# One gated load, two units later: the q load of batch 3 in pass w = 1 of a linear-attention and PReLU feed-forward kernel

## The chip, the cores and the metric

The kernel runs on one core of a Trainium2 chip. The metric is the device time of one execution in microseconds (us), the median of several runs on the same chip. Profiles come from one profiled execution each; a time such as "at 68.26" is us from the start of its span. PE is the matmul engine, PEld its weight loads, DVE the vector engine, ACT the scalar engine, POOL the GpSimd engine, SP the sync engine, which here only issues DMAs.

## The reference

For each of 8 batches and 8 heads of 64, with 576 rows each, attention without softmax is computed, then normalised over the head's 64 columns:

```
kv  = einsum('bhsd,bhse->bhde', k, v)
o   = einsum('bhsd,bhde->bhse', q, kv)
o   = o / sqrt(mean(o*o, -1) + 1e-6) * g_norm
x   = o laid out as (8*576 = 4608 rows) x (8*64 = 512 columns)
h   = x @ w_in                     # 512 -> 2048
g   = max(h, 0) + alpha * min(h, 0)
out = g @ w_out                    # 2048 -> 512
```

Inputs and output are float32. The kernel works in float16 with float32 accumulation.

## The kernel before, in words

**Blocks and passes.** The 4608 rows are cut into nine blocks of 512 rows, w = 0 to 8, each of four tiles of 128 rows. A block does not line up with a batch of 576 rows: block 2 (rows 1024 to 1535) takes its rows from batches 1 and 2, block 3 (1536 to 2047) its first 192 rows from batch 2 and the rest from batch 3. Block 0 is done by a start-up part of its own. The main loop at the end of the function (`for w in range(1, NW)`) makes passes w = 1 to 8, each of 16 units u. The change is in pass w = 1, the second of the nine blocks, here called loop 2 where they are counted from one.

**What a unit does.** Unit u of pass w multiplies xt of block w (the transposed attention output, four chunks of 128 x 512) with one 128-column block of w_in: four matmuls of 128 x 512 into a PSUM bank `h_ps` (`m1_mm`, L600). ACT takes Relu(-h) into `m_sb` (`m1_neg`, L609), DVE forms gt = h + beta * m_sb (`m1_sum`, L615). Then come matmuls of the second product (`prod_mm`, L796; yX, yY, yZ). They form a Strassen-like scheme on 2 x 2 halves, so DVE also adds and subtracts halves of gt (`s_sum`, L731 to L737) and of results (L828, L838, L840), and ACT copies results out (L824, L834). Results go to `y_sb` buffers, four in rotation, and are stored from there (L655) by POOL or SP.

**Attention of the next block.** Beside its own units, pass w makes xt of block w + 1, in `attention(w + 1, u)`, by a table `ROW_AT` written out by hand: at which unit the products k-transposed times v of a batch are formed (`row_kv`, L1122, with the masked copy L1134), at which the row matmuls of each tile (`rows_mm`, L499), the squares (L562 or L556), the reciprocal root (L572) and the scaling into `x_rows` on DVE (`rows_norm`, L580). Right behind L580, SP issues a DMA transpose of the tile into xt (L585). For block 2 the scalings of tiles 0, 1 and 3 stand at units 4, 9 and 9 of pass 1. Tile 2 of block 2 is made in column form (`cols_mm` L512, L522, L527, L534, and at unit 13 L541) and needs no transpose.

**The first unit of a pass.** From block 2 on, unit 0 is cut in two (`m1_cols`, L631): first the columns of tiles 0 to 2 (384), then, after second-product matmuls where the schedule has any, the columns of tile 3 (128). So the last transpose of a block may land a little after the pass has begun. In pass 2 the schedule has none of these between the two parts.

**q, k and v.** k and v are loaded by POOL with a cast to float16 into `kst` and `vst` (L176), with the last 64 rows of a batch in separate tiles (L198, `ksb`, `vsb`, `qsb`). From batch 3 on, q is loaded by `load_q` in four parts of 128 rows into `qst` (L185) and a fifth of 64 rows into `qsb` (L198). Each part is then transposed by an SP DMA into `qt_sb` (`dma_t`, L380); there are two `qt_sb`, for even and odd batches. Row matmuls read `qt_sb` as weights. The parts of batch 2 are transposed in pass 1 at units 0, 3, 3, 14 and 15; all five parts of batch 3 at units 0 to 2 of pass 2.

**What sets the order.** Each engine works through its instructions in the order in which this program writes them, and waits there for what they need. SP issues, in pass 1 and at the start of pass 2: the transposes of block 2's tiles, the last two parts of batch 2's q, the five of batch 3's q, then six stores of block 0's results that were held back (put at unit 5 of pass 2), then block 3's tiles. POOL issues loads and part of the stores. A load is held back by a gate: a copy of one element of a gt tile on POOL (L1186), which POOL cannot pass before DVE has written that gt. The table `LOADS` says at which unit of which pass a load is written, and its gate reads the gt of the unit before:

```python
        q, k, v = (11, 1, 1) if w == 1 else (12, 3, 5)
        for nm, at in (("q", q), ("k", k), ("v", v)):
            when = LOADS.setdefault((w + at // NF, at % NF), [])
            if at > 1 or w == 1:
                when.append(("gate", w, at - 1))
            when.append((nm, w + 2))
```

With w = 1 this is batch 3, with q at unit 11 behind the gt of unit 10; k and v stand at unit 1. In the later passes q stands at unit 12, k and v at units 3 and 5. Batch 2 is loaded by the start-up part.

Of the kernel before, what the change touches and what calls it, by code (L numbers as in the profile page):

```python
# [17 lines left out]
def kernel(  # L18
# [1168 lines left out]

    LOADS = {}
    for w in range(1, B - 2):
        q, k, v = (11, 1, 1) if w == 1 else (12, 3, 5)  # L1190
        for nm, at in (("q", q), ("k", k), ("v", v)):
            when = LOADS.setdefault((w + at // NF, at % NF), [])
            if at > 1 or w == 1:
                when.append(("gate", w, at - 1))
            when.append((nm, w + 2))
# [50 lines left out]
    w = NW - 1  # L1246
# [62 lines left out]
```

## Time and profile before

| | us |
|---|---|
| median of 3 runs | 274.43 |
| lowest and highest of them | 274.05, 274.45 |
| the profiled execution | 274.92 |
| its span, first to last instruction | 273.1 |
| PE, DVE, ACT busy | 265.7, 217.3, 156.4 |

The granted PE clock is 0.999 of full speed over the span. In the lists below, a line of a timeline has the start, the length and the instruction (with xN, N of them merged into one line), and in square brackets the idle time of its engine just before it with what ended that idle time. A line of the waits has the total, the number and the longest of the waits of one line on one cause. A line of the chain has start, length and what the time went to. The start and length of a DMA instruction on POOL or SP are those of its issue; when the data has landed is a time of its own, and "issue to landing" is the distance.

### The profile page before, as it was taken

The numbers are of one execution on the slowest core, as the hardware profiler recorded it, in microseconds if no ns is written. First come the engines' busy times: TensorE is split into PE (matmuls) and PEld (weight loads), VectorE is DVE, ScalarE is ACT, GpSimd is POOL, SyncE is SP. The second block draws the span as 40 slices with busy tenths as digits, with TensorE's granted clock in tenths as the row PEclk, the third lists the DMA queues.
The fourth block names the chain that finished last, engine by engine and source line by source line (L and its number), as shares of the span: only waits on it lengthen the run. The fifth ranks groups of instructions, "written<-read, shape, count | busy, mean of one in ns | idle before, by whom it ended". The sixth has DMA issues, their size and how long they took to land.

```text
span 273.1 us, 6175 instructions
## 1 busy us (share of the span) xinstructions
PE 265.7 (97%) x2286; PEld 168.5 (62%) x2286; DVE 217.3 (80%) x413; ACT 156.4 (57%) x532; POOL 87.6 (32%) x134
## 2 busy tenths in 40 slices
PE   7899999999799999999999999999999999999995
PEld 3354444456566676666666666676666666666684
DVE  6459658999768986998699869986998889778964
ACT  3467576785468546764675468546854864443410
POOL 8773461606251545154514341440110011101100
PEclk9999999999999999999999999999999999999999
DMA  8999999999989899959995999595051122211123
GB/s 160 197 202 202 195 199 193 178 182 108 161 159 204 132 166 148 153 113 172 135 144 130 151 135 158 137 143 111 19 134 43 41 44 90 61 40 40 40 77 119
DMA packets 91571, 35.59 MB, mean 130 GB/s; under 512 B 62980, under 2 KB 89748, under 8 KB 91540
## 3 DMA queue, kind: packets, MB, share of 16 engines
q0 software_dynamic: 57872, 23.83, 69.1%
q1 hardware_dynamic: 32628, 10.34, 22.4%
q10 hardware_dynamic: 1040, 1.02, 1.2%
q8 instruction: 18, 0.29, 0.4%
q14 instruction: 13, 0.11, 0.2%
HBM read 36.71 MB, written 9.44 MB: 169 GB/s over the span
## 4 chain that ended last, share of the span: by engine, by line
PE 79%; DMA 14%; DVE 2%; issue 1%; POOL 1%; ACT 1%; POOLq 0%
PE h_ps L600 35%; PE yY L796 15%; PE yZ L796 9%; PE yX L796 9%; DMA w_out_sb<-in_moe_w_out_dram 5%; PE y L643 4%; DMA xt<-x_rows 4%; DMA w_in_sb<-in_moe_w_in_dram 3%; DMA qst<-in_q_dram 2%; PE h_ps L631 2%; PE kv_ps L1122 2%; PE or_ps L499 2%; DVE gt L615 1%; DVE x_rows L580 1%; PE yZ L791 1%
## 5 line engine op out<-in xcount | busy, mean ns | idle before, releaser
L600 PE MATMUL h_ps<-xt,w_in_sb 128*128 128x512 f16 x540 | 136.2, 379 | 0.0
L609 ACT ACTIVATE m_sb<-h_ps 128x512 f32<-128x512 f32 x144 | 86.7, 603 | 81.9 <-PE h_ps L600 61.4
L615 DVE SCALAR_TENSOR_TENSOR gt<-m_sb,beta_sb,h_ps 128x512 f16<-128x512 f32 x144 | 106.2, 743 | 24.1 <-ACT m_sb L609 21.3
L600 PEld LDWEIGHTS <-w_in_sb 128*128 128x128 f16 x540 | 51.2, 98 | 39.4 <-issue 0.2
L655 POOL DMA_DIRECT2D out_dram<-y_sb x32 | 20.6, 646 | 123.3 <-DVE y_sb L838 57.1
L796 PEld LDWEIGHTS <-s 128*128 128x128 f16 x496 | 48.3, 98 | 11.3 <-DVE s L733 0.3
L796 PEld LDWEIGHTS <-gt 128*128 128x128 f16 x384 | 37.5, 98 | 23.2 <-issue 0.2
L796 PE MATMUL yX<-w_out_sb,gt 128*128 128x256 f16 x256 | 44.6, 273 | 0.0
L796 PE MATMUL yY<-wsum,s 128*128 128x256 f16 x256 | 35.2, 273 | 0.0
L562 ACT ACTIVATE sq_sb<-or_ps 128x64 f16<-128x64 f32 x144 | 30.9, 256 | 2.6 <-PE or_ps L499 2.6
L562 ACT ACTIVATION_READ_ACCUMULATOR sq_sb<-or_ps 128x1 f32 x144 | 30.3, 242 | 0.0
L580 DVE TENSOR_TENSOR x_rows<-or_ps,rstd_r 128x512 f16<-128x512 f32 x27 | 18.4, 684 | 1.0 <-ACT rstd_r L572 1.0
L828 DVE TENSOR_TENSOR u<-yY,p 128x512 f32<-128x512 f32 x16 | 11.0, 689 | 9.0 <-PE yY L796 9.0
L185 POOL DMA_DIRECT2D qst<-in_q_dram x20 | 17.7, 901 | 1.0 <-issue 1.0
L796 PE MATMUL yY<-wsum,gt 128*128 128x256 f16 x128 | 17.6, 272 | 0.0
L796 PE MATMUL yZ<-wsum,s 128*128 128x256 f16 x120 | 17.5, 272 | 0.0
L796 PE MATMUL yZ<-w_out_sb,s 128*128 128x256 f16 x120 | 16.7, 273 | 0.0
L643 PE MATMUL y<-w_out_sb,gt 128*128 128x512 f16 x64 | 16.3, 379 | 0.1
L731 DVE TENSOR_TENSOR s<-gt 128x512 f16<-128x512 f16 x32 | 13.3, 418 | 0.1
L733 DVE TENSOR_TENSOR s<-s,gt 128x512 f16<-128x512 f16 x32 | 12.8, 420 | 0.4
L737 DVE TENSOR_TENSOR s<-gt,s 128x512 f16<-128x512 f16 x32 | 12.7, 418 | 0.0
L735 DVE TENSOR_TENSOR s<-gt 128x512 f16<-128x512 f16 x32 | 12.4, 417 | 0.0
(107 smaller groups left out, 233.1 us busy)
## 6 DMA issues: line engine op xcount, KB each, us to landing
out_dram<-y_sb POOLq DMA_DIRECT2D x16, 256.0 KB, 2.7
kst<-in_k_dram POOLq DMA_DIRECT2D x7, 512.0 KB, 8.0
vst<-in_v_dram POOLq DMA_DIRECT2D x6, 512.0 KB, 7.9
qst<-in_q_dram POOLq DMA_DIRECT2D x20, 128.0 KB, 4.5
w_out_sb<-in_moe_w_out_dram POOLq DMA_DIRECT2D x8, 256.0 KB, 10.9
out_dram<-y_sb SPq DMA_DIRECT2D x5, 256.0 KB, 2.6
w_in_sb<-in_moe_w_in_dram POOLq DMA_DIRECT2D x2, 512.0 KB, 9.9
qst<-in_q_dram POOLq DMA_DIRECT2D x2, 512.0 KB, 11.9
```

The costliest lines, as they stand in the source:

```text
L185: nc.gpsimd.dma_start(out=st[:, t, :, :], in_=srcs["q"][b, :, t * P : (t + 1) * P, :].rearrange("h p d -> p h d"),)
L562: nc.scalar.activation(out=sq[:, half, j], in_=o_ps[:, half, j], func=AF.Square, accum_out=ssq[:, half, j : j + 1],)
L580: nc.vector.tensor_tensor(out=xr[:].rearrange("p j h d -> p h j d"), in0=o_ps, in1=rstd[:].unsqueeze(3).to_broadcast([P, 2, NPAIR, D]), op ...
L600: nc.tensor.matmul(out=h_ps[:], lhsT=w_in_blk(c, g), rhs=xts[w][:, c, :], start=(c == 0), stop=(c == NC - 1),)
L609: nc.scalar.activation(out=neg[w, g][:], in_=h_ps[:], func=AF.Relu, scale=-1.0)
L615: nc.vector.scalar_tensor_tensor(out=gts[w, i][:, r, :], in0=neg.pop((w, g))[:], scalar=beta_sb[:, g : g + 1], in1=h_ps[:], op0=ALU.mult, ...
L643: nc.tensor.matmul(out=y[:], lhsT=gt_cols(w, g, a * P, (a + 1) * P), rhs=w_out_blk(g), start=(n == 1), stop=(n == NF),)
L655: engs[store_turn[0] % len(engs)].dma_start(out=dst, in_=src)
L731: nc.vector.tensor_add(out=t[:], in0=a21, in1=a22)
L733: nc.vector.tensor_sub(out=t[:], in0=sums[w, 1, k][:], in1=a11)
L737: nc.vector.tensor_sub(out=t[:], in0=a12, in1=sums[w, 2, k][:])
L796: nc.tensor.matmul(out=bank, lhsT=lhs, rhs=rhs, start=fresh, stop=(c == NK - 1), skip_group_check=True,)
```

## The change

In the table `LOADS`, q of batch 3 is written at unit 13 of pass 1 instead of unit 11, and its gate reads the gt of unit 12 instead of unit 10. All that hangs on it is the gate copy, the four loads at L185 and the one at L198. Nothing else on POOL stands between units 11 and 13. In the program's order the load now stands after the last scaling of block 2 (unit 13) and before the transposes of batch 2's last two parts (units 14 and 15).

```diff
     LOADS = {}
     for w in range(1, B - 2):
-        q, k, v = (11, 1, 1) if w == 1 else (12, 3, 5)
+        q, k, v = (13, 1, 1) if w == 1 else (12, 3, 5)
         for nm, at in (("q", q), ("k", k), ("v", v)):
             when = LOADS.setdefault((w + at // NF, at % NF), [])
             if at > 1 or w == 1:
                 when.append(("gate", w, at - 1))
             when.append((nm, w + 2))
```

## The prediction

> **What bounds the kernel now.** I read the page first, then the waits of the matmul queue, then the chain, and last the timelines of PE, SP, POOL and DVE around the place of the change. Times are microseconds from the start of the profiled execution.
>
> ```profile
> PE 265.7 (97%) x2286; PEld 168.5 (62%) x2286; DVE 217.3 (80%) x413; ACT 156.4 (57%) x532; POOL 87.6 (32%) x134
> ```
>
> PE is busy for 97% of the span, so only two things shorten this kernel: fewer matmuls, or fewer holes between them. The edit changes no matmul. The holes are few; this is the whole list of what PE waited for, total, times, longest:
>
> ```profile
> PE h_ps L631 <- DMA xt<-x_rows: 1.6, 1, 1.6
> PE warm_ps L297 <- DVE y_sb L119: 1.5, 1, 1.5
> PE kv_ps L403 <- ACT qt_sb L361: 0.8, 1, 0.8
> PE ssq_ps L460 <- ACT sq_sb L444: 0.2, 1, 0.2
> ```
>
> The last three are in the first 15 us. The largest is one wait of 1.6 at L631, where unit 0 of a pass multiplies the last 128 columns, those of tile 3. The chain and PE's timeline place it at the start of pass w = 2:
>
> ```profile
> 63.95 5.83 DMA xt<-x_rows
> 69.78 0.04 issue
> ```
>
> ```profile
> 67.45 0.81 PE L631 MATMUL h_ps<-xt,w_in_sb 128*128 128x384 f16 x4
> 69.83 0.38 PE L631 MATMUL h_ps<-xt,w_in_sb 128*128 128x128 f16 x4 [1.56 <-DMA xt<-x_rows]
> ```
>
> The first 384 columns end at 68.26; then PE stands for 1.56 until the transpose of tile 3, issued at 63.95, has landed at 69.78, 5.83 after its issue. POOL and SP show what it shared the DMA engines with:
>
> ```profile
> 62.87 0.18 POOL L1186 COPY gate_sb<-gt 1x1 f16<-1x1 f16 x1 [8.04 <-DVE gt L615]
> 63.36 3.58 POOL L185 DMA_DIRECT2D qst<-in_q_dram  x4 [0.32 <-issue]
> 66.91 0.73 POOL L198 DMA_DIRECT2D qsb<-in_q_dram  x1
> 73.33 2.14 POOL L655 DMA_DIRECT2D out_dram<-y_sb  x4 [5.70 <-ACT y_sb L834]
> ```
>
> ```profile
> 55.67 9.50 SPq L585 DMA_TRANSPOSE xt<-x_rows  x3
> 65.22 3.19 SPq L380 DMA_TRANSPOSE qt_sb<-qsb  x2
> 68.66 5.39 SPq L380 DMA_TRANSPOSE qt_sb<-qst  x4
> 74.15 1.21 SPq L380 DMA_TRANSPOSE qt_sb<-qsb  x1
> 75.41 4.26 SPq L655 DMA_DIRECT2D out_dram<-y_sb  x6
> ```
>
> The q load goes out at 63.36, 0.59 ahead of the transpose. In the DMA view by slices of 1 us, POOL's queue has 1 packet in 64 to 65, 437 in 65 to 66, 553, 804 and 959 in the next three; SP's queue has 46, 1, 391, 140 and 116. So the transpose finds the engines taken when its packets come up, at about 66.
>
> **The change, part by part.** Nothing is added or removed, and the order of instructions on every engine stays the same. The copy at L1186 now reads gt of unit 12 instead of unit 10, and five loads stand behind it on POOL (four of L185, one of L198).
>
> *How far it moves.* DVE's L615 for units 10 and 11 fills 61.99 to 63.39; unit 12 is the one at 63.64, 0.74 long, so done at 64.38. With the 0.14 that the copy took after its gt before, it starts at about 64.52, which is 1.65 later. The loads are then issued from 65.01 to 69.3 instead of 63.36 to 67.64, and their packets begin near 66.7 instead of 65.0. "Two units" is 1.65 us here: the load is issued 1.06 behind the transpose instead of 0.59 ahead.
>
> *What the transpose then takes.* No row has exactly this distance, so I bound it. Below: 2.4, issue to landing, for the same transpose of the pass that has no q load (203.12). Above: the passes where a q load is issued 0.16 behind the same transpose, 3.8 (120.12) and 3.6 (175.41). That is landing at 66.4 to 67.8. PE needs it at 68.26, so all of the 1.56 goes, with 0.5 to spare. I take the end near 3.6, since a load is near.
>
> The row first: most of tile 3's data packets are through by 67.5 (391 + 140 of SP's packets by 68, some of them the next transpose's), yet it counts as landed at 69.78. The Trainium skill (DMA: Bandwidth & Descriptors, Queues, rings and completion order) says that an engine takes turns among its queues by packet, and that a completion increment lands only after all earlier writes of that engine, those of other queues too. By turns alone the wait should have been shorter than measured; by the rule on increments, q writes still hold a landing if they begin before it. By the first the sum keeps 1.56, by the second part of it can stay; this is the first rival below.
>
> *What moves up behind the hole.* PE's next work is kv (k and v landed by 63.4) and unit 1. DVE is the nearest limit:
>
> ```profile
> 68.07 0.75 DVE L731 TENSOR_TENSOR s<-gt 128x512 f16<-128x512 f16 x2
> 68.74 0.75 DVE L733 TENSOR_TENSOR s<-s,gt 128x512 f16<-128x512 f16 x2
> 70.88 0.75 DVE L615 SCALAR_TENSOR_TENSOR gt<-m_sb,beta_sb,h_ps 128x512 f16<-128x512 f32 x1 [1.39 <-ACT m_sb L609]
> ```
>
> The sums end at 69.49 whatever PE does, so DVE moves up by 1.39, not 1.56. Unit 2's matmuls move from 72.86 to 71.3 and need gt of unit 0, then done at 70.2; the sums that PE takes from about 72.2 are done at 71.0 and 71.8. So PE is not held, and the 0.17 is made up where DVE idles later (1.10 at 78.14, 1.13 at 80.35). I count 1.5, between 1.39 and 1.56.
>
> *What becomes late.* On POOL the next instruction is the store at 73.33, which waits for ACT; the loads end at 69.3, so nothing queues. On SP the four transposes of L380 each wait for their own part of q: in the rows they start within 0.15 us of its landing. They move by 1.65 to about 70.3 to 75.8, and the six stores behind them from 75.41 to 77.1, ending at 81.3. SP's next is block 3's first transpose, 84.18 before and 82.6 when moved up with PE: 1.3 to spare. PE's first use of the new q is the row matmul of unit 4, 78.27 before and 76.7 after. Batch 3's first transpose landed 5.0 after its issue at 68.66, at 73.7; 1.65 later is 75.3, so 1.4 to spare. Parts 1 and 2 of q (transposed by 74.6, then 76.2) are used from 80.25, then 78.7: 2.5 to spare. The cover of the move is this slack; without it each us costs one us on PE.
>
> Two y_sb buffers change places as well: the sum at L840 near 95.4 takes the one stored by POOL from 73.33 (landed by 79.2), the copy at L834 of pass 2 the one stored last by SP (landed by 85.7, then 87.3). Both are needed after 93, so this costs nothing.
>
> *Later passes* keep their distances, since their gates, norms and loads follow PE. Block 3's tile 3 is issued at 92.53; its increments end at 96.8 and its use is at 98.07, so 1.3 is left.
>
> **Sum.** 0 + 1.5 gained, 0 lost. The profiled execution took 274.92 (span 273.1 and 1.8 around it); the median is 274.43, 0.49 below. I take the difference from both: 273.4 for the one, **272.9** for the median.
>
> **Rivals.**
>
> 1. *The hole only shrinks.* The load still begins 1.6 ahead of PE's need, and its writes hold the landing. For it: 5.83 beside it before, and the 4.5 of the transpose at 231.08, which had no q load. Against: 3.6 and 3.8 with the load closer. At 5.0 (batch 3's first transpose, mid-load) tile 3 lands at 68.95 and 0.7 of the hole stays: gain 0.8, 273.6.
> 2. *The hole moves.* The DMA work of 65 to 90 starts 1.65 later while PE comes 1.56 earlier, and the next such place, block 3's tile 3 with 1.3 to spare, stalls. All 1.56 lost there needs 2.9 of delay. For it: the DMA engines are nearly full from 80 to 89. Against: they carry nothing from 90.3 to 91.5. Time 274.4, no change.
> 3. *Slower: the row matmuls of unit 4 wait for q.* The place is PE's L499; it decides when batch 3's first transpose lands after 76.7. The longest landing of a transpose beside a large load in this trace is 8.9 (issued 55.67, under the k and v loads). Issued at 70.3 it would land at 79.2, PE would stand for 2.5, and the net is 0.95 worse: 275.4. Against: the rows beside this very load are 5.0, 3.9 and 3.2.
>
> **How the numbers follow.** Forecast 0.76, own range 272.5 to 273.4 (1.39 to 1.56 gained, 0.4 either way for scatter and small leftovers; the three runs lie within 0.4). Rival 1 0.10, rival 2 0.06, rival 3 0.08. The range takes in the forecast and rival 1, 272.4 to 273.9, and leaves out 0.14. A measurement of this kernel can tell 0.2%, 0.55 us, from no change: faster means below 273.9, which the forecast and rival 1 give, 0.86; same 0.06; slower 0.08.
>
> **What would show it.** The L1186 copy near 64.5 and the loads from 65.0 show the move. L631's wait gone from PE's list, and tile 3 landing within 4.0 of its issue, show the gain; a landing of 4.5 to 5.5 is rival 1. A wait of L631 near 96 is rival 2; a wait of L499 near 77 is rival 3. It would be wrong altogether if tile 3 landed as late as before with the load out of its way: then the k and v loads, or the transposes among themselves, were the cause.

## The result, and the profile after

The changed kernel takes 273.38 us (median of 22 runs), the kernel before 274.36 in the same comparison: ratio 0.9962, 95% interval 0.9949 to 0.9975, so 1.0 faster. Two later comparisons of the same two kernels gave 0.9984 (0.9964 to 1.0004) and 0.9978 (0.9961 to 0.9995), that is 0.4 and 0.6; the ratio is that of the means, and the first of these two intervals reaches 1. The profiled execution after has a span of 271.7 against 273.1.

The page's first line, after: no busy time has changed by more than 0.2, but PE's same work fills 98% of a shorter span.

```profile
PE 265.6 (98%) x2286; PEld 168.5 (62%) x2286; DVE 217.3 (80%) x413; ACT 156.2 (58%) x532; POOL 87.4 (32%) x134
```

All that PE waited for, after (total, times, longest). The wait of L631 is gone; what is left is start-up:

```profile
PE warm_ps L297 <- DVE y_sb L119: 1.5, 1, 1.5
PE kv_ps L403 <- DMA vst<-in_v_dram: 1.1, 1, 1.1
PE ssq_ps L460 <- ACT sq_sb L444: 0.2, 1, 0.2
```

PE's timeline after, where the two parts of unit 0 now run into each other and are listed as one line of eight matmuls:

```profile
67.85 1.04 PE L631 MATMUL h_ps<-xt,w_in_sb 128*128 128x384 f16 x8
```

POOL and SP after. The start-up part ran 0.40 later in this execution (this L631 was at 67.45 before), so 64.92 stands for 64.52:

```profile
64.92 0.18 POOL L1186 COPY gate_sb<-gt 1x1 f16<-1x1 f16 x1 [9.68 <-DVE gt L615]
65.42 3.59 POOL L185 DMA_DIRECT2D qst<-in_q_dram  x4 [0.32 <-issue]
72.01 2.14 POOL L655 DMA_DIRECT2D out_dram<-y_sb  x4 [2.31 <-ACT y_sb L834]
```

```profile
70.21 5.24 SPq L380 DMA_TRANSPOSE qt_sb<-qst  x4
75.56 2.42 SPq L380 DMA_TRANSPOSE qt_sb<-qsb  x1
78.03 3.79 SPq L655 DMA_DIRECT2D out_dram<-y_sb  x6
82.85 9.55 SPq L585 DMA_TRANSPOSE xt<-x_rows  x4
```

Tile 3's transpose was issued at 64.37 and landed at 66.79, 2.42 later instead of 5.83. In the list of issues with their time to landing, window 65 to 66, it stands as:

```profile
xt<-x_rows SPq DMA_TRANSPOSE x1, 2.4
```

What each queue moved between 67 and 68, after (packets, MB, share of the 16 engines): it is the first slice of 1 us with packets of the q load, and tile 3 has landed by then.

```profile
q0 software_dynamic: 344, 0.04, 68.0%
q1 hardware_dynamic: 101, 0.03, 19.6%
```

Set side by side by matmul, PE's starts are 0.40 behind before's up to L631, then 1.32 ahead: 1.72 from the hole. This is more than the 1.56 of idle time, because the end of a matmul in the profile lies about 0.17 behind the point at which the next one can start: before, the fifth matmul of L631 could have started at 68.09 and started at 69.83. They stay 1.3 ahead up to pass 8, where before lost another 0.28 to a late landing at L631 that a second trace of before does not have. The end is 1.59 ahead.

### The profile page after: what moved, and what is told of

Same layout as the page of the kernel before. It is cut to its first block, busy times and chain, and to the rows that moved or that the text cites. A ratio compares the mean times of both kernels' runs of the same rounds, so it can differ in the third digit from the quotient of the medians.

```text
span 271.7 us, 6175 instructions
## 1 busy us (share of the span) xinstructions
PE 265.6 (98%) x2286; PEld 168.5 (62%) x2286; DVE 217.3 (80%) x413; ACT 156.2 (58%) x532; POOL 87.4 (32%) x134
## 4 chain that ended last, share of the span: by engine, by line
PE 94%; DMA 3%; POOL 1%; issue 1%; ACT 0%; DVE 0%; POOLq 0%
PE h_ps L600 44%; PE yY L796 16%; PE yX L796 10%; PE yZ L796 10%; PE y L643 5%; DMA vst<-in_v_dram 3%; PE h_ps L631 2%; PE kv_ps L1122 2%; PE or_ps L499 2%; PE ssq_ps L460 1%; PE yZ L791 1%; PE h_ps L945 1%; POOL kst L168 0%; PE ot_ps L437 0%; PE kv_ps L418 0%
## 5 line engine op out<-in xcount | busy, mean ns | idle before, releaser
L615 DVE SCALAR_TENSOR_TENSOR gt<-m_sb,beta_sb,h_ps 128x512 f16<-128x512 f32 x144 | 106.3, 744 | 22.4 <-ACT m_sb L609 19.3
L185 POOL DMA_DIRECT2D qst<-in_q_dram x20 | 17.7, 906 | 1.0 <-issue 1.0
```

What stands on the lines that cost most here:

```text
L185: nc.gpsimd.dma_start(out=st[:, t, :, :], in_=srcs["q"][b, :, t * P : (t + 1) * P, :].rearrange("h p d -> p h d"),)
L615: nc.vector.scalar_tensor_tensor(out=gts[w, i][:, r, :], in0=neg.pop((w, g))[:], scalar=beta_sb[:, g : g + 1], in1=h_ps[:], op0=ALU.mult, ...
```

## The experiments

My theory: the hole is the landing of tile 3's transpose, held up by packets of a q load issued ahead of it; it goes as soon as those come later, and the only other edge is where the row matmuls want q. Rivals: the gain is proportional to the shift; the hole only moves to L499; something other than PE's wait is saved. The time of each kernel is a median, beside the runs of before in the same comparison.

### The two kernels again

No edit. First pair:

> The kernel before, unchanged, timed against itself: it shows what the comparison calls no change, and whether the hole of 1.56 at L631 is the same in another execution. The medians so far differ by 0.98 (273.38 against 274.36), the profiled executions by 1.48. If the hole varies from run to run, this profile has a hole clearly other than 1.56 (0.8 to 1.3 would explain the 1.0); if the hole is fixed, it is again 1.5 to 1.6, and the missing 0.5 was given back by the changed kernel or lies in the 0.49 by which the first profiled execution was above its median. Time: within 0.3 of before.

> The changed kernel, unchanged. If its gain is kept, L631 has no wait again, tile 3's transpose lands 2.4 to 3 after its issue, and no other wait of PE appears; the time is 1.0 to 1.5 below before. If part is given back from run to run, a wait of L499 appears near 79, where the second group of row matmuls takes the third part of batch 3's q, which landed at 78.49 in the first profile for a use at 78.92, 0.43 to spare; then the span is 0.2 to 1 longer than 271.7.

Second pair, one of them with the row matmuls moved as further below:

> The kernel before once more, for another trace and more times. The holes at L631 seen so far are 1.57, 1.58 and 1.36 (the last with the later row matmuls). If the hole is as steady as that, this one is 1.3 to 1.6, and the change should be worth 1.3 on the mean of many runs. If the hole is smaller in many executions, which would explain gains of 0.4 to 1.0 in the comparisons, it shows here or in the next.

> The change once more. Two traces gave no wait of L631 and a wait of L499 of 0 and 0.30. If L499 takes back a varying part, this trace has a wait there between 0 and 1; the mean gain over this comparison is then 0.8 to 1.3. If neither L631 nor L499 waits and the gain is still below 1, the rest lies in what varies from run to run elsewhere (start-up, first landing of w_out), which no edit here touches.

> As before_3: a hole of 1.3 to 1.6 at L631 if it is steady; the time within 0.3 of before.

Before against itself: 273.96 beside 273.99, ratio 0.9994 (0.9973 to 1.0016); 274.13 and 274.14 beside 273.85, 1.0011 (0.9991 to 1.0031) and 1.0010 (0.9995 to 1.0025). The change: 273.30 beside 273.99, and 273.11 beside 273.85. The waits of L631 in before_again, before_3 and before_4, one line from each:

```profile
PE h_ps L631 <- DMA xt<-x_rows: 1.6, 1, 1.6
```

```profile
PE h_ps L631 <- DMA xt<-x_rows: 0.4, 1, 0.4
```

```profile
PE h_ps L631 <- DMA xt<-x_rows: 1.4, 1, 1.4
```

So the hole is not steady: with the first profile, 1.56, 1.58, 0.41 and 1.42 in four executions of the same kernel; by the starts of its matmuls PE lost 1.74, 1.74, 0.58 and 1.59. I had taken it for steady, and before_3 refutes that. In before_3, SP spent 2.09 on issuing tile 1's transpose instead of 2.35 to 2.54, tile 3 was issued only 0.33 behind the first part of q instead of 0.6 to 0.8, and it landed in 4.94 instead of 5.5 to 5.8 (the last section tells what that issue time goes with). The change has no wait of L631 in any trace. It has a new one in one of three (after_again, PE's waits):

```profile
PE or_ps L499 <- DMA qt_sb<-qst: 0.3, 1, 0.3
```

### q one unit later

```diff
-        q, k, v = (11, 1, 1) if w == 1 else (12, 3, 5)
+        q, k, v = (12, 1, 1) if w == 1 else (12, 3, 5)
```

> q of batch 3 at unit 12, behind the gt of unit 11: issued at about 64.0, 0.1 behind the transpose of tile 3 instead of 0.6 ahead (before) or 1.05 behind (after). Theory of contention: what counts is whose packets come first; with the load 0.16 behind, other passes landed in 3.6 and 3.8, so tile 3 lands near 67.7, before PE's 68.26, and the hole goes: 273.4, as the change. Rival, that the gain is proportional to the shift of the load: a third of it, a hole of about 1.0 is left and the time is near 274.0.

273.40 beside 273.99, ratio 0.9977 (0.9953 to 1.0001). Tile 3 and the first part of q are issued at the same time, 63.93; tile 3 lands in 4.18, at 68.11, and PE's eight matmuls are one line again:

```profile
67.37 1.17 PE L631 MATMUL h_ps<-xt,w_in_sb 128*128 128x384 f16 x8
```

They take 1.17 instead of the 1.04 of the change: the fifth starts at 68.15 where 68.02 was possible, so 0.13 of the hole is left, too short for the list of waits. The proportional rival expected a hole of about 1.0. The interval of the time reaches that rival's 274.0; it is the trace that decides against it. The landing itself does fall with the distance: 5.83 and 5.73 with q 0.6 and 0.7 ahead, 4.94 at 0.33 ahead, 4.18 at 0, 2.42 at 1.05 behind. A longer lead did not make it longer still: with q 0.77 to 0.79 ahead, in three traces, it was 5.45 to 5.50. PE's need at about 4.1 after the issue makes a threshold of it.

### q four units later

```diff
-        q, k, v = (11, 1, 1) if w == 1 else (12, 3, 5)
+        q, k, v = (15, 1, 1) if w == 1 else (12, 3, 5)
```

> q of batch 3 at unit 15, behind the gt of unit 14: issued at about 67.5, 2.5 later than with the change in before's time base, about 2.1 later counted in PE's units. The hole at L631 stays away. If the row matmuls are the other edge, the third part of q then lands transposed 2.1 later, near 80.6 where the second group of L499 wants it at 78.9, PE waits 1.2 to 2.0 there, and the time is back at 274 to 275. By my own prediction, with 2.5 to spare there, it would be the same as the change, 273.4.

274.36 beside 273.99, ratio 1.0013 (0.9993 to 1.0034), 1.1 above the change's 273.30 of that comparison. PE's waits and its timeline at L499:

```profile
PE or_ps L499 <- DMA qt_sb<-qst: 1.8, 1, 1.8
```

```profile
76.24 0.20 PE L499 MATMUL or_ps<-kv_masked,qt_sb 64*128 64x64 f16 x2
78.21 0.49 PE L499 MATMUL or_ps<-kv_masked,qt_sb 64*128 64x64 f16 x22 [1.77 <-DMA qt_sb<-qst]
80.15 0.41 PE L499 MATMUL or_ps<-kv_masked,qt_sb 64*128 64x64 f16 x16
```

The hole has moved from L631 to L499, with the size expected, but at the first group: two matmuls on batch 2's columns, then 1.77 until batch 3's first part, issued at 70.70, lands at 78.16 (7.46). I had expected it at the second group.

### The row matmuls two units later

```diff
-        {4: ((1, 0),), 5: ((3, 2),)}, 'sq': (4, 4, 5, 6, 8, 8, 8, 9), 'rs': (6, 6, 10, 11), 'norm':
+        {4: ((1, 0),), 7: ((3, 2),)}, 'sq': (4, 4, 5, 6, 8, 8, 8, 9), 'rs': (6, 6, 10, 11), 'norm':
```

With the change (twice), and with the kernel before as a control:

> The changed kernel with the second group of block 3's row matmuls (tiles 3 and 2) at unit 7 of pass 2 instead of unit 5, so that the third part of batch 3's q is wanted about 3.7 later (near 82.7 instead of 78.9). If the missing 0.3 to 0.5 of the gain is given back in the wait of L499, that wait is gone in every execution, and the time is 0.2 to 0.5 below the change (273.3 in the last comparison): 272.8 to 273.1, 1.1 to 1.5 below before. If the shortfall has another cause, it stays at 0.7 to 1.0 below before.

> The control: the kernel before with the same shift of the row matmuls to unit 7 and q still at unit 11. Before, the third part of q landed at 74.4 for a use at 80.2, so nothing waits there; by the theory of the L499 wait this is the same as before within 0.3, with the hole of 1.56 to 1.58 at L631. If it is faster too, the shift helps for another reason than that wait.

> The change with the second row matmuls of block 3 at unit 7, once more. If the wait of L499 is what the change gives back, this is the fastest of the four, 1.1 to 1.5 below before and 0.2 to 0.4 below the change, with no wait of PE after the start-up part. So far it was 0.6 below before by medians, 0.8 by means, no better than the change; if it is again no faster than the change, the wait of L499 costs too little to be measured.

With the change 273.29 beside 273.90, ratio 0.9960 (0.9938 to 0.9982), and 273.16 beside 273.85, 0.9979 (0.9962 to 0.9996). The control is 274.42 beside 273.90, ratio 0.9995 (0.9969 to 1.0021), with a hole of 1.36 at L631. No trace of the first two has a wait of L499 or L631, yet they are no faster than the change: 273.16 against 273.11 in the one comparison that has both. The wait of L499 is real, and too rare or short to be measured here. Nothing shows that the rest of the gain went there, but with intervals of nearly 0.5 either way a share of 0.2 or 0.3 cannot be ruled out.

### The hole covered, not removed

```diff
             if late:
+                if w == 2:
+                    row_kv((3,))
                 m1_cols(h_ps, w, u, W - P, W)
...
-        7, 8), 'rs': (3, 9, 10, 9), 'norm': (4, 9, 13, 9), 'red': (1, 1, 0, 1)}, 3: {'kv': 0, 'mm':
+        7, 8), 'rs': (3, 9, 10, 9), 'norm': (4, 9, 13, 9), 'red': (1, 1, 0, 1)}, 3: {'kv': 99, 'mm':
```

> The kernel before, q at unit 11, with the 40 kv matmuls of batch 3 (L1122, 0.75 of PE) put between the two parts of unit 0 of pass 2, into the hole instead of behind it. If the hole on PE is the whole cost of the early load, tile 3 still lands 5.7 to 5.8 after its issue, the wait shrinks from 1.57 to about 0.8, and the time falls by 0.75 to 273.2 to 273.4. If the early load costs by something else than PE's wait for this landing, the time stays within 0.3 of before.

273.62 beside 273.90, ratio 0.9980 (0.9956 to 1.0005). By the time alone this does not decide between 0.75 and nothing. The trace, of one execution, does: tile 3 still lands 5.46 after its issue, and the wait is down by the kv work in front of it, from the 1.38 that it would be with it behind:

```profile
70.05 0.38 PE L631 MATMUL h_ps<-xt,w_in_sb 128*128 128x128 f16 x4 [0.63 <-DMA xt<-x_rows]
```

PE was 0.44 behind before_again ahead of pass 2 and 0.41 ahead of it from unit 3 to the end, so 0.85 was gained there and kept: 0.75 of kv work covered, and a hole that was itself 0.1 to 0.2 smaller in this execution.

### The change without four stores

```diff
+        if w == 1 and what == "c11":
+            return
         quad_out(w, int(what[1]) - 1, int(what[2]) - 1, y_sb, subs)
```

> The changed kernel without the four stores of the first result quarter of block 1, which POOL issues at about 71.7 to 73.8 (this part of the output is left out). In two profiles of the change the third part of q took 5.6 and 6.4 from issue to landing, beside these stores, and 3.2 before, where the stores came after it. If the stores hold it up, it lands 3 to 4 after its issue, near 76.4, and L499 does not wait. If it is held up by the k load of batch 4 (issued from 75.1) or by the other transposes, it takes 5.5 to 6.5 again.

One execution, 273.54; the kernel leaves out that part of the output. The third part of q lands 4.41 after its issue, at 77.96, between the two expectations; the second part takes 2.61 instead of 3.85 to 4.16. Both were also issued 0.6 to 0.7 later than in the first profile of the change, counted from the start of pass 2, so their landings moved less than these times: 0.5 and 0.6 sooner. If this one execution is typical, the stores are part of what holds up the transposes there, and not all of it. What else does was not settled. In the packet records the k load of batch 4 begins at the same time, and with it come packets of 128 to 256 bytes that take 300 to 900 ns instead of 20 to 30. A second candidate stands just ahead of them: a packet of 16 KB on the instruction queue, 75.92 to 76.85. In the three traces of the change it runs between 75.2 and 77.1, behind the issue of the third part; in the four of the kernel before it begins only after that part has landed. No run here moves one without the other.

## Why the prediction was right, and where it was not

**The mechanism held.** The load moved by the 1.65 worked out (copy at 64.92 less 0.40; the loads 1.05 behind the transpose, for 1.06 predicted), and the wait of L631 went. The landing came out at the lower end of my bounds, 2.42 and not 3.6: in the seven traces with q issued 0.96 or more behind the transpose it is 2.42 or 2.43. I took the end of the nearer row; the right row was the pass without a q load, because packets of q start 1.6 after its issue and meet nothing.

**The rule on increments.** With q's packets under way, tile 3's 16 completion increments arrived over 68.49 to 69.78; with none they came within 66.68 to 66.79. The trace agrees with what the Trainium skill says (DMA: Bandwidth & Descriptors, Queues, rings and completion order), that an increment lands only after the earlier writes of its engine on all queues. The packet records show that a plain sharing of the engines is not all of it. On SP's queue such a transpose is 512 packets of 256 bytes and 32 of 4 bytes. Before, counted in the queue's order, tile 3's 512 had all begun by 67.8, ahead of PE's need near 68.1, and the last of its 32 at 68.20; the last increment came 1.58 after that. With the change that distance was 0.34. That the writes of q are what held the increments is not shown: with q at unit 12, where q's packets were under way too, the last increment came 0.31 after the last packet.

**DVE** moved up as counted: after, L615 follows the last of the sums at 69.81 (69.41 on before's clock, 69.49 predicted) and PE was not held. My 1.5 stood between DVE's 1.39 and the idle 1.56; PE's starts gained 1.72 at once, so DVE was no limit.

**The size was off: "so all of the 1.56 goes".** All of it went, but it was one execution's hole. With the four traces of the kernel before, the mean is 1.24 of idle time, or 1.41 by the starts of the matmuls, and the third is 0.41 (0.58). The gain was measured as 1.0, 0.7 and 0.7 by medians (1.0, 0.4 and 0.6 by ratio), where I said 1.5 for a median of 272.9. A mean loss of 1.41 less a mean wait of 0.1 at L499 would give 1.3. Where the remaining 0.3 to 0.9 went is open: whether untraced executions of before have smaller holes still was not traced. The kernel before scatters more (272.6 to 276.5 over 157 runs, against 272.7 to 275.0 over 46), as a varying hole would make it; that this is the reason is not shown.

**What was luck.** By its time alone, 273.38 lies at the upper end of my own range and nearer to the 273.6 of rival 1 than to 272.9; it is the trace, with a landing of 2.42 and no wait of L631, that tells the two apart. The profiled execution came out at 273.44 for 273.4, but as a sum of other terms: the hole gave 1.72, pass 8 another 0.28, and the later start-up took 0.40 of it back.

**The slack of q was off: "2.5 to spare".** I moved the landing of part 2, the third one, by the 1.65 of its load, to 76.2. After, it landed at 78.49 for a use at 78.92, and in after_again 0.3 too late. Its transpose took 5.6 and 6.4 instead of 3.2. Its issue, 1.5 later, now falls beside POOL's four stores, which had themselves come 1.3 earlier with PE; the run without them suggests that they are a part of the cause, and the rest is open. For the first part 1.4 were predicted, and 2.8 were there (74.12 for 76.95).

**The rivals.** Rival 1 did not happen. Rival 2 did not either: block 3's L631 does not wait after. Rival 3 named the right line and, as q at unit 15 shows, the right edge for a load that is moved further: there a landing of 7.5 beside the load makes a hole of 1.77, and the whole gain is lost. Its own price, a landing of 8.9, a hole of 2.5 and 275.4, was too high even for that. With the change itself L499 waited in one trace of three, 0.30, and at the second group.

## What to carry to other kernels

When a transfer lands late although it was issued in time, look at what was issued on the other queues just ahead of it; moving a large load that nobody is waiting for behind it can be worth the whole wait, and here the distance that mattered was less than 1 us: with q issued 0.6 ahead of the transpose PE's next matmul started 1.74 late, with q issued at the same time 0.13 late. Such a move has an edge on the other side, and its slack must be worked out with the moved transfers' new neighbours, not with their old durations. A hole that hangs on how two queues meet is not one number: take it from several traces before counting on it.

## What the runs showed of the hardware that I had not expected

- A DMA transpose of 128 x 512 landed in 2.42 or 2.43 in all seven traces in which no packet of q came before its landing; the same one with a cast load of 4608 packets of 128 bytes issued ahead of it took from 4.94 to 5.83 in six traces.
- A transfer whose packets have all begun can still count as landed much later: before, tile 3's last packet began at 68.20 and its last increment came at 69.78.
- SP's issue of tile 1's transpose took 2.04 to 2.54 from trace to trace, where those of tiles 0 and 3 take 1.2. In all 14 traces it ended 0.42 or 0.43 after the end of a packet of 16 KB on the instruction queue, itself 1.4 to 2.1 long, and tile 3 was issued 0.09 behind it. So the end of that packet goes with how far ahead q gets, and with the size of the hole. That SP waits there for this packet is a reading of the traces that no run tested.
